# Sliding-window attention and dropless MoE on one core: another division of the queries, score groups issued in pairs, a third task list in three portions

## The chip, the cores and the metric

The kernel runs on one core of one Trainium2 chip. The metric is the device time of one execution in microseconds (us), taken as the median of several runs; before the change it was 678.85 us over five runs (677.37 to 681.30). A profile is one further execution, recorded by the hardware profiler. Engines are called by the profile's short names: PE is TensorE's matmul queue and PEld its weight loads, DVE is VectorE, ACT ScalarE, POOL GpSimd and SP SyncE. "L828" is line 828 of the kernel before.

## The reference

Attention with a window of 128 keys and a bias that falls with distance is followed by a mixture of eight experts, of which each token takes one. All data are float32: 8 batches, 8 heads, 576 positions, head size 64; 4608 tokens of width 512; experts with a hidden width of 1024.

```python
def _attn_ref(q, k, v):
    scores = scale * np.matmul(q, k.transpose(0, 1, 3, 2))
    bias = slopes[:, None, None] * (-np.abs(rel).astype(np.float32))[None, :, :]
    mask = (rel >= 0) & (rel < window)
    scores = np.where(mask, scores + bias[None], -1000000000.0)
    attn = np.exp(scores - np.max(scores, axis=-1, keepdims=True))
    attn = attn / (np.sum(attn, axis=-1, keepdims=True) + 1e-09)
    return np.matmul(attn, v)

def _moe_ref(x, w_gate, w1, w2):
    logits = x @ w_gate
    expert_idx = np.argmax(logits, axis=1)
    probs = softmax(logits)
    gate_w = probs[np.arange(N), expert_idx]
    for e in range(E):                       # rows sorted by expert
        h = np.maximum(x_sorted[lo:hi] @ w1[e], 0.0)
        y_sorted[lo:hi] = h @ w2[e]
    return gate_w[:, None] * y
```

## The kernel before

The work has two stages. In the first, attention runs over 16 *units*: a unit is one pair of heads of one pair of batches, and four units in a row (four pairs of heads) make up one pair of batches, called `bp` 0 to 3. Behind each pair of batches its tokens are routed: gate products, a choice of expert, and rows written to DRAM (`x_rows`) sorted later by a gather. In the second stage the experts' matmuls run, with a Strassen scheme. The order of the instructions on every engine is written out by hand: an engine works through its queue in the order in which the Python code issues, and waits where a semaphore isn't there yet.

A sequence of 576 positions has nine blocks of 64 keys, and a key block meets at most three query blocks (its own and the next two). For a unit the loop at L1389 takes four steps, `g` = 0 to 3; the step counter over all units is `i`. The pieces are:

- `scores(i)`: the score products of one step's key blocks (two blocks, or three at `g` = 3; L785, 16 or 24 passes of weight load and matmul), into one of two PSUM buffers `sp`; then ACT's exponentials (L794, L804) and DVE's product with the bias factors (L798), into one of six buffers `pe`. `scores_to(n)` issues groups up to number n, so scores run three (units 0 and 1) or four steps ahead of their use.
- `values(u, half, kbs)`: the products of probabilities and values (L828) for key blocks `kbs`, for one half of the queries. The halves are `QH`: query blocks 0 to 4 and 5 to 8. There is one PSUM buffer `at` for them, so a half's first product waits until the half before has been copied.
- `finish(u, half)`: ACT copies the half's context to `xT` (L845, L847); PE forms the row sums (L859) in a PSUM buffer `m`, and DVE adds them to `sumT` (L870), or ACT copies them there for the first pair of heads (L868). There are two `m` buffers, taken in turn by everything outside scores and values.
- `some()`: pops one portion of tasks. `behind(bp)` returns the list of portions for a finished pair of batches, and the loop appends it after the pair's last step. Its members: `gate` (L879, with DVE's sum L884 or L886), `turn` (a PE transpose L903 and ACT's copy L904), `scale_a` to `scale_c` and `count` (small DVE operations), `place` and `place2` (L990 to L1014), `ones_at` and `ones_at2` (one-hot tables on DVE, L1023, L1029, L1038), `enlist` (L1048). Rows of the later pairs are turned on PE (`row_turned`, L1067, with ACT's copy L1069 into one of four `xs` buffers) and written by POOL (`row_out`, L1076 and L1081). Rows of the first pair are transposed on DVE (`squares_turned`, L1118, into the same `xs` buffers) and written by POOL in four DMAs each (`squares_scaled` L1126, `squares_out` L1137), after `scales_squared` (L1096, L1104).
- For `bp` = 2 the last portion also gathers the first expert's rows (L1271), and the last unit's steps scale and turn them (`to_scale` L1283, `to_columns` L1296).

Loads of unit u + 2 are issued on SP, one in each step. Ahead of each stands a tiny DMA that reads `prob[i + 1]` (`no_earlier_than`, L638), so the load can't start before that score group has been made.

Of the kernel before, what the change touches and what calls it, by code (L numbers as in the profile page):

```python
# [458 lines left out]
def kernel(  # L459
# [22 lines left out]
    KB = P // 2  # L482
# [24 lines left out]
    with ExitStack() as fast:  # L507
# [67 lines left out]

        GC = 384
        LQ = 4 * P
        QH = [(0, 5 * KB), (5 * KB, 4 * KB)]

        ac = pool(att, "att_consts", 1)  # L580
        qk = pool(att, "qk", 3)
# [227 lines left out]
        def by_distance(x, kb, a, b):  # L809

            if kb == NK - 1:
                return x[:, 5 * KB :].rearrange("p (j x) -> p j x", j=1)
            return x.rearrange("p (j k x) -> p j k x", j=3, k=2)[:, a:b, kb % 2, :]

        def values(u, half, kbs):

            bp, hp = units[u]
            q0, qn = QH[half]
            if (u, half) not in at:
                at[u, half] = ps_a.tile([P, 2, 512], F32, name="at"), set()  # L820
            acc, begun = at[u, half]
            for kb in kbs:
                pe = prob[4 * u + min(kb // 2, 3)]
                lo, hi = max(q0, kb * KB), min(q0 + qn, (kb + 3) * KB)
                at_kb = (kb, lo // KB - kb, hi // KB - kb)
                for c in range(2):
                    for r in range(2):
                        nc.tensor.matmul(  # L828
                            acc[r * D : (r + 1) * D, c, lo - q0 : hi - q0].rearrange("p (j x) -> p j x", x=KB),
                            lhsT=v_sb[u][c * KB : (c + 1) * KB, kb, r * D : (r + 1) * D],  # L830
                            rhs=by_distance(pe[c * KB : (c + 1) * KB, r, :], *at_kb),
                            start=(c, r) not in begun, stop=True, skip_group_check=True,
                        )
                        begun.add((c, r))

        def finish(u, half):

            bp, hp = units[u]
            q0, qn = QH[half]
            if hp == 0 and half == 0:  # L840
                xT[bp] = xp.tile([P, HP, 2 * S], F32, name="xT")
                sumT[bp] = xp.tile([P, S], F32, name="sumT")
            acc = at.pop((u, half))[0]
            n = min(q0 + qn, LQ) - q0
            nc.scalar.copy(xT[bp][:, hp, : 2 * LQ].rearrange("p (b q) -> p b q", b=2)[:, :, q0 : q0 + n], acc[:, :, :n])  # L845
            if n < qn:
                nc.scalar.copy(xT[bp][:, hp, 2 * LQ :].rearrange("p (b q) -> p b q", b=2), acc[:, :, n:qn])  # L847
            sm = ps_m.tile([P, 512], F32, name="m")
            ops = []
            for kb in range(max(0, q0 // KB - 2), (q0 + qn) // KB):  # L850
                lo, hi = max(q0, kb * KB), min(q0 + qn, (kb + 3) * KB)
                ops.append((kb % 2, lo, hi, prob[4 * u + min(kb // 2, 3)], (kb, lo // KB - kb, hi // KB - kb)))
            if half == 0:
                ops.insert(0, (1, 0, KB, None, None))
            begun = set()
            for par, lo, hi, pe, at_kb in ops:
                for r in range(2):
                    j = 2 * r + par
                    nc.tensor.matmul(  # L859
                        sm[32 * j : 32 * j + 32, lo - q0 : hi - q0].rearrange("p (j x) -> p j x", x=KB),  # L860
                        lhsT=none[:] if pe is None else ind[:, hp, :],
                        rhs=fac[:, 0:1, :KB] if pe is None else by_distance(pe[:, r, :], *at_kb),
                        start=j not in begun, stop=True, skip_group_check=True,
                    )
                    begun.add(j)
            to = sumT[bp][:, q0 : q0 + qn]
            if hp == 0:
                nc.scalar.copy(to, sm[:, :qn])  # L868
            else:
                nc.vector.tensor_tensor(to, sm[:, :qn], to, op=ALU.add)  # L870
# [212 lines left out]
        def row(bp, t):  # L1083
            row_turned(bp, t)
            row_out(bp, t)
# [30 lines left out]
        def squares_turned(bp, t):  # L1116
            xs = squares(bp, t)
            nc.vector.transpose(  # L1118
                xs[:, :, :PD].rearrange("p k (h j) -> p k h j", h=HP),
                xT[bp][:, :, t * P : (t + 1) * P].rearrange("p h (k i) -> p k h i", k=NA),  # L1120
            )
# [218 lines left out]
        def behind(bp):  # L1340

            g3 = [lambda k=k: gate(bp, k) for k in range(3)]
            t3 = [lambda k=k: turn(bp, k) for k in range(3)]
            rs = [lambda t=t: row(bp, t) for t in range(TPB)]
            a, a2, b, b2, c, n, q, p, p2, o, o2, e = (
                [lambda f=f: f(bp)] for f in (
                    scale_a, scale_a2, scale_b, scale_b2, scale_c, count, scales_squared, place, place2, ones_at,
                    ones_at2, enlist,
                )
            )  # L1350
            if bp == 0:
                rt = [lambda t=t: squares_turned(bp, t) for t in range(TPB)]
                ro = [
                    lambda t=t: (squares_scaled(bp, t), squares_out(bp, t, nc.gpsimd)) for t in range(TPB)
                ]
                return [g3[0:1], g3[1:2], g3[2:] + t3[0:1], t3[1:], a, a2, b, b2, c + n, rt[0:1], q + p + rt[1:2],
                        p2 + rt[2:4] + ro[0:2], o + ro[2:4], o2, rt[4:6] + ro[4:5], e + rt[6:8] + ro[5:8]]
            rt, ro = ([lambda t=t, f=f: f(bp, t) for t in range(TPB)] for f in (row_turned, row_out))
            if bp == 1:
                last = [lambda: squares_turned(0, TPB - 1), lambda: squares_scaled(0, TPB - 1),  # L1360
                        lambda: squares_out(0, TPB - 1, nc.gpsimd)]
                return [g3[0:1], g3[1:2], g3[2:] + t3[0:1] + last, t3[1:], a + rt[0:1], a2 + rt[1:2], b + rt[2:3],
                        b2 + rt[3:4], c + n, [], p + ro[0:2], p2 + ro[2:4] + rs[4:5], o + rs[5:6], o2 + rs[6:7], rs[7:8],
                        e + rs[8:9]]
            return [g3, t3, a + a2, b + b2 + rt[0:1], c + n + rt[1:2], rt[2:4], p + p2 + ro[0:4], o + o2 + rs[4:6],
                    rs[6:9] + [early_holes], e + [early_table, lambda: gather(fixed[0], x_d[: 3 * 2 * S, :])]]

        tasks = []
# [1 line left out]
        def some():  # L1370
            if tasks:
                for f in tasks.pop(0):
                    f()
# [4 lines left out]
        def scores_to(n):  # L1378
            while scored[0] < min(n, NG):
                scores(scored[0])  # L1380
                scored[0] += 1
# [7 lines left out]
        for i in range(NG):  # L1389
            u, g = divmod(i, 4)  # L1390
            bp, hp = units[u]
            if u + 2 < len(units):
                no_earlier_than(prob[i + 1][0:1, 0, 0:1])
                load_part(u + 2, g)
            if u in (5, 6) and g % 2 == 1:
                d = 2 * (u - 5) + g // 2
                load_w1(fixed[0], w1_a, slice(d, d + 1))
            if i == 1:
                token_numbers()
                table_consts()  # L1400
            if i == 12:
                token_parts()

            ahead = i + (3 if u < 2 else 4)
            if g == 0:
                scores_to(ahead)
            if g == 0:
                values(u, 0, (0, 1))
                if u < HP - 1:
                    factors(u + 1)  # L1410
            elif g == 1:
                values(u, 0, (2, 3))
            elif g == 2:
                values(u, 0, (4,))
                finish(u, 0)
                some()
                scores_to(ahead)
                values(u, 1, (3, 4, 5))
            else:
                values(u, 1, (6, 7, 8))  # L1420
                finish(u, 1)
            if u in (10, 11):
                ws_tasks.pop(0)()
            if u == len(units) - 1 and g == 1:
                first = [t for _, t in prepare(fixed[0])]
                tasks.extend(first[:3])
            if g != 2:
                some()
            if g in (1, 3):
                scores_to(ahead)  # L1430
            if g == 3 and hp == HP - 1 and bp < BP - 1:
                tasks.extend(behind(bp))
# [250 lines left out]
        for i in range(len(groups)):  # L1683
            g = groups[i]
# [20 lines left out]
            ahead = []  # L1705
# [47 lines left out]
```

## Time and profile before

| | |
|---|---|
| median of five runs | 678.85 us (677.37 to 681.30) |
| the profiled execution | 678.02 us, span 676.3 us |
| granted TensorE clock | 0.999 |
| PE busy | 650.8 us, 96% |
| DVE, ACT, POOL busy | 362.0, 215.6, 238.9 us |
| DMA | 122.01 MB, 180 GB/s over the span |
| last score product starts, last value product of attention | about 163 and 169 us |

A row of the timeline gives the start, the duration, the engine, the line and operation, the tiles, how many instructions were merged, and in square brackets the idle time of the engine before it with what ended it ("issue" is none that the profile shows). A row of the stage windows gives the stretch, its length, then busy time and instruction count of PE, PEld, DVE, ACT and POOL, the granted clock, the DMA share and GB/s. Matmul durations include the pipeline's drain, so gaps on PE show more plainly in the weight loads' rows.

### The profile page before, as it was taken

What the parts mean: (1) busy time and instruction counts of PE and PEld (TensorE: products, weight loads), DVE (VectorE), ACT (ScalarE), POOL (GpSimd) and SP (SyncE); (2) the same over time, 40 slices, a digit from 0 to 9 for tenths busy, and PEclk for the clock granted to TensorE, in tenths of its full rate; (3) what the DMA queues carried; (4) which work ended last, traced back from release to release, by engine and by line L of the source; (5) the groups of instructions that cost most, each with busy time, mean ns of one, the idle gap of its engine ahead of it and who ended that gap; (6) DMA issues with size and microseconds to landing.
All of it is one profiled execution on the core that took longest, in us unless ns stands there. A gap on an engine that the chain in (4) does not pass through costs nothing.

```text
span 676.3 us, 14663 instructions
## 1 busy us (share of the span) xinstructions
PE 650.8 (96%) x6004; PEld 542.5 (80%) x6004; DVE 362.0 (54%) x727; ACT 215.6 (32%) x493; POOL 238.9 (35%) x372
## 2 busy tenths in 40 slices
PE   6899889999999999999999999999999999999995
PEld 5777768687788888978878887889788888878893
DVE  3345848776697768435633761484257436623510
ACT  5657557676331231023102311310231023113200
POOL 8000573215032571247026521732371266112020
PEclk9999999999999999999999999999999999999999
DMA  9876997965438944582386518444823664184010
GB/s 274 215 205 189 330 238 215 295 183 165 143 85 266 339 131 141 185 286 68 118 269 215 169 52 289 155 154 157 304 59 135 227 246 149 53 288 151 1 63 9
DMA packets 63167, 122.01 MB, mean 180 GB/s; under 512 B 5905, under 2 KB 29489, under 8 KB 63090
## 3 DMA queue, kind: packets, MB, share of 16 engines
q1 hardware_dynamic: 51138, 92.51, 43.0%
q0 software_dynamic: 10800, 27.58, 12.7%
q8 instruction: 49, 0.80, 0.5%
q10 hardware_dynamic: 1152, 0.88, 0.4%
q14 instruction: 28, 0.23, 0.1%
HBM read 101.79 MB, written 19.96 MB: 180 GB/s over the span
## 4 chain that ended last, share of the span: by engine, by line
PE 67%; issue 15%; POOL 6%; DVE 4%; DMA 2%; ACT 1%; SPq 0%; POOLq 0%; DVEq 0%; ACTq 0%
PE sp L785 4%; PE at L828 4%; PE pair1a L1558 4%; PE pair1b L1558 4%; PE pair0b L1501 4%; PE pair0a L1501 4%; PE pair0a L1558 4%; PE pair0b L1558 4%; PE pair2b L1501 4%; PE pair2a L1501 4%; POOL xg L1271 4%; PE pair1b L1501 3%; PE pair1a L1501 3%; PE pair2b L1558 3%; PE pair2a L1558 3%
## 5 line engine op out<-in xcount | busy, mean ns | idle before, releaser
L1271 POOL DMA_INDIRECT xg<-x_rows,p_idx x124 | 125.4, 1011 | 37.8 <-issue 37.2
L1581 POOL DMA_INDIRECT out_dram<-zo,s_idx x39 | 44.4, 1139 | 244.5 <-DVE zo L1572 142.8
L798 DVE TENSOR_TENSOR pe<-pe,fac 128x512 f32<-128x512 f32 x64 | 43.6, 687 | 45.6 <-ACT pe L794 45.6
L785 PE MATMUL sp<-q_sb,k_sb 64*64 64x192 f32 (+2 forms) x1152 | 55.9, 322 | 9.3 <-DMA q_sb<-in_qT_dram 5.0
L828 PE MATMUL at<-pe,v_sb 64*64 64x192 f32 (+2 forms) x1408 | 56.2, 287 | 2.9 <-issue 2.0
L828 PEld LDWEIGHTS at<-pe,v_sb 64*64 64x64 f32 x1408 | 47.0, 135 | 11.6 <-issue 4.6
L785 PEld LDWEIGHTS sp<-q_sb,k_sb 64*64 64x64 f32 x1152 | 40.6, 137 | 18.3 <-issue 7.6
L794 ACT ACTIVATE pe<-sp 128x512 f32<-128x512 f32 x64 | 38.5, 601 | 32.8 <-issue 18.5
L804 ACT ACTIVATE pe<-sp,mid 128x128 f32<-128x128 f32 x128 | 40.2, 374 | 0.0
L1512 ACT ACTIVATE h<-h 128x512 f32<-128x512 f32 x32 | 20.2, 630 | 38.6 <-DVE h L1511 38.6
L859 PE MATMUL m<-pe,ind 128*32 128x192 f32 (+2 forms) x704 | 29.7, 286 | 1.1 <-DVE sumT L870 0.9
L1137 POOL DMA_DIRECT2D x_rows<-xs x48 | 26.0, 549 | 9.7 <-POOL xs L1126 2.3
L1283 DVE TENSOR_TENSOR xn<-xg 128x512 f32<-128x512 f32 x39 | 26.2, 675 | 1.3 <-DMA xg<-x_rows,p_idx 0.7
L859 PEld LDWEIGHTS m<-pe,ind 128*32 128x32 f32 x704 | 23.1, 109 | 3.7 <-DVE sumT L870 1.0
L1299 DVE STREAM_TRANSPOSE xgT<-xn 128x512 f32<-128x512 f32 x31 | 22.0, 711 | 1.1
L845 ACT COPY xT<-at 128x640 f32<-128x640 f32 (+1 forms) x32 | 18.9, 591 | 9.4 <-PE at L828 6.6
L538 DVE TENSOR_TENSOR w2s<-w 128x512 f32<-128x512 f32 x16 | 11.0, 685 | 20.3 <-DMA w<-in_moe_w_dram 20.3
L1126 POOL COPY xs<-sq 128x16 f32<-128x16 f32 x10 | 2.6, 264 | 54.0 <-ACT sq L1104 54.0
L1613 PE MATMUL pair2a<-w,h 128*128 128x512 f32 x48 | 21.1, 592 | 0.0
L1501 PE MATMUL pair0a<-xgT,w 128*128 128x256 f32 x72 | 17.1, 380 | 0.0
L1501 PE MATMUL pair0b<-xgT,w 128*128 128x256 f32 x72 | 17.1, 380 | 0.0
L1558 PE MATMUL pair1a<-w,h 128*128 128x256 f32 x72 | 17.1, 380 | 0.0
(378 smaller groups left out, 1382.9 us busy)
## 6 DMA issues: line engine op xcount, KB each, us to landing
w<-in_moe_w_dram SPq DMA_DIRECT2D x29, 2048.0 KB, 7.8
k_sb<-in_kT_dram SPq DMA_DIRECT2D x15, 576.0 KB, 5.9
q_sb<-in_qT_dram SPq DMA_DIRECT2D x15, 576.0 KB, 5.4
v_sb<-in_v_dram SPq DMA_DIRECT2D x30, 288.0 KB, 5.9
x_rows<-xs POOLq DMA_DIRECT2D x16, 264.0 KB, 4.6
x_rows<-xs POOLq DMA_DIRECT2D x32, 66.0 KB, 5.6
x_rows<-xT SPq DMA_DIRECT2D x8, 264.0 KB, 5.9
w<-in_moe_w_dram SPq DMA_DIRECT2D x4, 512.0 KB, 9.6
```

The lines of the kernel that those rows point to most:

```text
L785: nc.tensor.matmul(by_distance(sp[c * KB : (c + 1) * KB, r, :GC], kb, 0, n), lhsT=k_sb[u][hs, c, kb * KB : (kb + 1) * KB], rhs=q_sb[u][hs, ...
L794: nc.scalar.activation(outer, sp[:, :, :GC].rearrange("p r (j x) -> p r j x", j=3)[:, :, 0:3:2, :], AF.Exp, scale=SCALE,)
L798: nc.vector.tensor_tensor(outer, outer, fac[:, h0 : h0 + 2, : 2 * w].rearrange("p r (j x) -> p r j x", j=2)[:, :, :, : 2 * KB], op=ALU.mult,)
L804: nc.scalar.activation(pe[:, r, inner], sp[:, r, inner], AF.Exp, bias=mid[:, h0 + r : h0 + r + 1], scale=SCALE,)
L828: nc.tensor.matmul(acc[r * D : (r + 1) * D, c, lo - q0 : hi - q0].rearrange("p (j x) -> p j x", x=KB), lhsT=v_sb[u][c * KB : (c + 1) * KB, ...
L859: nc.tensor.matmul(sm[32 * j : 32 * j + 32, lo - q0 : hi - q0].rearrange("p (j x) -> p j x", x=KB), lhsT=none[:] if pe is None else ind[:, ...
L1137: eng.dma_start(x_d[r0 : r0 + n * m, a * PW : (a + 1) * PW].rearrange("(k i) w -> i k w", i=TQ), xs[a * TQ : (a + 1) * TQ, p0 // TQ : p0 / ...
L1271: nc.gpsimd.indirect_dma_start(out=to, out_offset=None, in_=where, in_offset=bass.IndirectOffsetOnAxis(ap=idx, axis=0),)
L1283: nc.vector.tensor_tensor(xn[:], x, s.unsqueeze(3).to_broadcast([P, NA, HP, TQ]), op=ALU.mult)
L1501: nc.tensor.matmul(ps[:, f * 256 : (f + 1) * 256], lhsT=left[m][:, d, fb * P : (fb + 1) * P], rhs=right[m][:, d, :], start=(m in (1, 2, 5) ...
L1558: nc.tensor.matmul(ps[:, :256], lhsT=left[m][:, f, c * P : (c + 1) * P], rhs=right[m][:, f, :], start=(m in (1, 2, 5) and f == 0), stop=Tr ...
L1581: ins = nc.gpsimd.indirect_dma_start(out=out[:, :], out_offset=bass.IndirectOffsetOnAxis(ap=s_idx[:, g["c0"] + j : g["c0"] + j + 1], axis= ...
```

## The change

The queries are divided behind four blocks in place of five, so the first half needs key blocks 0 to 3 only and the second needs 2 to 8. `finish(u, 0)` moves from step 2 to step 1, ahead of that step's portion, and step 2's portion moves behind its scores and values. The score group of step 2 now directly follows that of step 1, as that of step 0 already followed that of step 3. In the list of the second pair (`bp` = 1) the last row of the first pair, left over in `last`, moves from the third portion to the first. The list of the third pair (`bp` = 2) gets three portions in place of two for the gate products and turns, so every later portion comes one step later.

```diff
-        QH = [(0, 5 * KB), (5 * KB, 4 * KB)]
+        QH = [(0, 4 * KB), (4 * KB, 5 * KB)]
...
-                return [g3[0:1], g3[1:2], g3[2:] + t3[0:1] + last, t3[1:], a + rt[0:1], a2 + rt[1:2], b + rt[2:3],
+                return [g3[0:1] + last, g3[1:2], g3[2:] + t3[0:1], t3[1:], a + rt[0:1], a2 + rt[1:2], b + rt[2:3],
                         b2 + rt[3:4], c + n, [], p + ro[0:2], p2 + ro[2:4] + rs[4:5], o + rs[5:6], o2 + rs[6:7], rs[7:8],
                         e + rs[8:9]]
-            return [g3, t3, a + a2, b + b2 + rt[0:1], c + n + rt[1:2], rt[2:4], p + p2 + ro[0:4], o + o2 + rs[4:6],
+            return [g3[0:2], g3[2:] + t3[0:1], t3[1:], a + a2, b + b2 + rt[0:1], c + n + rt[1:2], rt[2:4], p + p2 + ro[0:4], o + o2 + rs[4:6],
                     rs[6:9] + [early_holes], e + [early_table, lambda: gather(fixed[0], x_d[: 3 * 2 * S, :])]]
...
-            if g == 0:
+            if g % 2 == 0:
                 scores_to(ahead)
             if g == 0:
                 values(u, 0, (0, 1))
...
             elif g == 1:
                 values(u, 0, (2, 3))
+                finish(u, 0)
             elif g == 2:
-                values(u, 0, (4,))
-                finish(u, 0)
-                some()
-                scores_to(ahead)
-                values(u, 1, (3, 4, 5))
+                values(u, 1, (2, 3, 4, 5))
             else:
                 values(u, 1, (6, 7, 8))
                 finish(u, 1)
...
-            if g != 2:
-                some()
-            if g in (1, 3):
+            some()
+            if g % 2 == 1:
                 scores_to(ahead)
```

## The prediction

> **What bounds the kernel now.** I read the busy shares first, then the windows by stage, the waits of the weight loads, and the timeline of attention.
>
> ```profile
> PE 650.8 (96%) x6004; PEld 542.5 (80%) x6004; DVE 362.0 (54%) x727; ACT 215.6 (32%) x493; POOL 238.9 (35%) x372
> ...
> 70.00:85.00 15.00, 12.89 (x311) 10.79 (x310) 12.12 (x28) 8.71 (x24) 9.90 (x21) 1.00 1.05 325
> ...
> 175.00:190.00 15.00, 14.71 (x77) 12.79 (x76) 10.64 (x33) 6.08 (x12) 0.00 (x0) 1.00 0.24 91
> ...
> PEld sp L785 <- issue: 6.9, 14, 1.9
> PEld at L828 <- issue: 4.6, 9, 1.1
> PEld at L828 <- ACT xT L845: 2.5, 7, 0.4
> ```
>
> TensorE sets the end in every stage. After 173 us (experts) it has almost no gap, and the diff touches nothing there; what can change lies in attention, 4 to 173 us. A matmul's row includes its drain, so I read gaps from the weight loads. Between 30 and 175 us they wait 2.5 us for the context copies (L845), which is what the change is near. More, 11.5 us, is "issue": part is the 0.17 us between groups of another array shape, but seven of them stop in the middle of a group with no semaphore (ending at 22.84, 30.03, 35.45, 66.96, 73.46, 79.45, 84.64; 0.44 to 1.91 us, together 7.7). The instruction queue moves 49 packets, 0.80 MB, so 16 KB each, about 245 of the 12,008 PE instructions; from 66.96 to 73.46 lie 129 pairs of load and matmul. I read these as PE waiting for its next instruction packet behind data (DMA share 1.05 in that window).
>
> **1. The gap at the division, gain.** One unit without other tasks:
>
> ```profile
> 41.91 0.53 PEld L785 LDWEIGHTS sp<-q_sb,k_sb 64*64 64x64 f32 x16
> ...
> 42.08 0.70 ACT L845 COPY xT<-at 128x640 f32<-128x640 f32 x1
> ...
> 42.83 1.41 PEld L828 LDWEIGHTS at<-pe,v_sb 64*64 64x64 f32 x48 [0.39 <-ACT xT L845]
> ```
>
> The second half's values reuse the only context buffer, so they wait for the copy; row sums (0.9) and one score group (0.53) cover it and leave 0.39. After the change two score groups lie there: 0.53 more cover, and a copy of 512 instead of 640 elements (0.60 by the 128x512 copies of L904, against 0.70). ACT first has the exponentials of two groups to do, 1.0 us each by their spacing at 46.10 and 47.09, from 1.0 us after the pair of scores starts: copy done 3.8 us after it, values due at 1.31 + 1.14 + 0.75 + 1.06 = 4.3. The gap closes. (Units 1 and 2 have 0.86 us of factors on ACT ahead of the copy: 0.3 may stay.) SP issues the same DMAs in the same order, POOL too but for the gather of step 4. The same total of blocks is multiplied: per unit 88 value and 48 sum matmul passes before and after. The other copy grows from 0.48 to 0.60; sums and two scores (2.1) still hide it, and if not it costs 0.12 a unit.
>
> The gap stands in eight units (14.48, 34.36, 42.83, 62.06, 82.14, 95.80, 138.90, 160.97; 0.28 to 0.39, together 2.84). In units 0, 2, 5 and 7 a packet wait follows within some 5 us and takes the gain back: PE arrives 0.36 earlier at a packet that comes no earlier. Units 8, 12 and 14 are in the sums below. Left: unit 3, **-0.4**.
>
> *Rule against trace.* The Trainium skill, "Runtime: NRT & Kernel Launch", section "Instruction fetch mechanics", says that crossing a 16 KiB block is mostly hidden. Here 7.7 us were not. By the rule those four gaps are gained too, 1.4 us more; I follow the trace.
>
> **2. Unit 8, loss.** A portion at g = 2 stood after the fifth block and the first sums; now it stands after two scores and four blocks of values. Of the first pair the tenth portion there (scales squared, L1096) starts POOL's row writes: first copy at 71.74, then DMAs whose waits reach back eight DMAs. DVE's transposes of later rows wait for those landings, and PE for DVE:
>
> ```profile
> 87.63 0.71 DVE L1118 STREAM_TRANSPOSE xs<-xT 128x512 f32<-128x512 f32 x1 [1.90 <-DMA x_rows<-xs]
> ...
> 90.24 0.71 DVE L1118 STREAM_TRANSPOSE xs<-xT 128x512 f32<-128x512 f32 x1 [1.89 <-DMA x_rows<-xs]
> ...
> 91.58 0.34 PE L828 MATMUL at<-pe,v_sb 64*64 64x64 f32 x8 [0.52 <-DVE pe L798]
> ...
> 92.78 0.25 PE L859 MATMUL m<-fac,none 128*32 128x64 f32 x2 [0.86 <-DVE gs L884]
> ```
>
> The chain starts later by score 0.53 + values 1.14 + array change 0.17 = 1.85. Bounds: 0 (the chain takes it up elsewhere) and 3.5 (the packet wait that ended at 73.46 then falls ahead of L1096; by my count of pairs it falls just behind). I take 2.2. So the row 7 transpose moves from 90.24 to 92.4, and behind it on DVE two factor products and the first gate's sum; PE, now held by the second gate product, which needs the first one's PSUM buffer, goes on at 92.78 + 2.2. From there before needed 6.11 to the next pair of scores (98.89). After: second gate 1.06, two scores 1.23, values 1.14, third gate 0.47, turn 0.45, values 1.02, sums 0.92, two turns 0.75 = 7.04, since fewer pieces were done ahead of the wait: +0.93. The last row's transpose, two portions earlier, waits on DVE for row 4's landing with the second gate's sum behind it; the unit's context copy waits for that transpose before (95.06) and after. It ends before PE's values ask. Its 8 DMAs stay last on POOL. **+3.1**.
>
> *Rule against trace.* "DMA: Bandwidth & Descriptors", section "Anatomy of one DMA — SWDGE (gpsimd) path", fits 2.0 us plus bytes over 436 GB/s: 2.15 us for the 66 KB of a piece. The row of these DMAs says 5.6. By the rule no transpose would wait and this loss would be nothing; I follow the row.
>
> **3. Units 10 and 11.** Placing (L990) waits 0.82 for DVE in unit 10; two pieces later it finds its input ready. But in unit 11 the sums now stand between rows 5 and 6, so row 6 needs row 5's copy, which ACT delays (it stood 2.03 us for a row buffer at 119.35). Between -0.8 and +0.2: **-0.3**.
>
> **4. Third pair.** Three portions shift all later ones by one slot. Unit 12: the 0.39 gap and 0.24 of the turns' wait go; two more array changes (0.35) and 0.2 for the first turn, which needs ACT's copy of the sums, come. Slot 8 (unit 14, g = 0) gets the one-hot tables:
>
> ```profile
> 151.97 0.60 DVE L1023 TENSOR_TENSOR at_col<-cols_b,rc 128x432 bf16<-128x432 bf16 x1
> ...
> 152.60 1.13 DVE L1029 TENSOR_TENSOR oc<-at_col,tok 128x432 bf16<-128x432 bf16 x2
> ...
> 153.64 1.35 DVE L1038 TENSOR_TENSOR gsr<-cols_b,rc 128x1152 bf16<-128x1152 bf16 x1
> ...
> 166.91 0.69 DVE L1283 TENSOR_TENSOR xn<-xg 128x512 f32<-128x512 f32 x1 [0.40 <-DMA xg<-x_rows,g_idx]
> ```
>
> These 3.0 us now precede the first sums' add on DVE. Counted from the pair of scores: factor products end at 3.35, tables 6.4, add 6.85. PE has finished row 6 at 5.0; row 7 needs the sums' buffer (two `m` buffers alternate) and waits 1.85. Behind it: row 8, the hole product (0.35 for row 7's copy), both scores, all values. In unit 15 no scores are left to cover the division: 0.5. F0 waits 0.1, array changes 0.15. The gather goes out about 1.7 us later, but the product that uses it moves behind four blocks of values: the wait of 0.76 goes, with 0.38 (row 8) and 0.34 (unit 14's gap). +3.5 - 2.1 = **+1.4**; with the tables done earlier -0.4, with ACT later +2.5.
>
> **Sum:** -0.4 + 3.1 - 0.3 + 1.4 = +3.8. The profiled execution took 678.02 (span 676.3 and 1.7 around it), 0.8 under the median; 681.8 there, **682.7** as a median.
>
> **Rivals.** *A, as summed*, 0.55; own range 680.4 to 685, more above than below since the 3.5 of step 2 lies upward. *B, the row chain takes up its delay*, 0.17: POOL stood 2.30 us at 79.70, which the trace puts down to DVE's at_col; if that, not the landing, held it, 2.2 goes: 680.5. Against it: that DMA's wait names the first row's landing as well, and 7.2 us is the longest landing in the view. *C, faster*, 0.15: in unit 8 DVE never waits for a landing. The price of that place is then its old waits, 0.86 + 0.99 gained; with eight gaps 2.8, L990 0.8, minus 1.4 for the third pair: 673.8 to 675. It decides once landings stay under about 3.5 us (2.9 is the shortest seen); against it stands a median of 5.5 from 60 to 100 us. *D, packets later still*, 0.13: the loads are paced by probabilities, which now come in twos, so two loads start together; if each of the seven packet waits grows by 0.8, +5.6: 688.
>
> **Chances.** A measurement here can tell some 0.5% (3.4 us). A lies beyond in 0.41 and within in 0.14; B is within; C faster; D slower. Faster 0.15, same 0.31, slower 0.54. Leaving out most of C and part of D gives 677 to 687.5.
>
> **What would show it.** No wait on L845 ahead of values in units 3 and 5; L1126's first copy about 2 us later against L828 of unit 6, and the second gate product of unit 8 waiting 3 us or more on L884; a row turn (L1067) of unit 14 waiting near 1.9 us on sumT L870. Wrong if DVE's transposes stop waiting for landings, or if packet waits shrink or move. After 175 us nothing should differ.

## The result, and the profile after

The changed kernel took 682.7 us, the median of 30 runs (678.3 to 688.26), beside 679.07 us for the kernel before (56 runs): a ratio of 1.0055, 95% interval 1.0041 to 1.0069. So it is slower by half a per cent, and the prediction's 682.7 us is what came. The sum behind it is another matter: two of its terms were wrong, and one cause was not in it at all. (Here and below, a ratio leaves out runs of over 1.5% above the fastest of their kernel: four of twelve in one kernel, named there, and none elsewhere.) The profiled execution took 682.47 us (span 680.7; 678.02 and 676.3 before).

The busy shares of the kernel after, from the page:

```profile
PE 653.3 (96%) x6004; PEld 544.7 (80%) x6004; DVE 363.4 (53%) x727; ACT 216.5 (32%) x493; POOL 238.9 (35%) x372
```

The same two stretches as before, in the windows view (stretch, length, busy time and instructions of PE, PEld, DVE, ACT, POOL, granted clock, DMA share, GB/s):

```profile
70.00:85.00 15.00, 12.35 (x287) 10.25 (x290) 12.34 (x28) 6.78 (x19) 9.95 (x21) 0.92 1.05 314
175.00:190.00 15.00, 14.70 (x91) 11.21 (x90) 9.97 (x23) 5.84 (x11) 0.00 (x0) 1.00 0.42 141
```

The number to see is 0.92. Before, the clock column of this stretch read 1.00. And the waits of the weight loads between 30 and 180 us (wait, sum, times, longest):

```profile
PEld at L828 <- issue: 5.0, 15, 0.8
PEld m L859 <- issue: 4.0, 3, 2.4
PEld m L879 <- DVE gs L884: 3.6, 2, 2.7
PEld m L1067 <- DVE sumT L870: 2.3, 2, 1.7
...
PEld at L828 <- ACT xT L845: 0.6, 1, 0.6
```

The wait for the context copies (L845) went from 2.5 us in seven places to 0.6 in one, the last unit. In its place stand two long ones: 2.7 us at a gate product and 1.7 us at a row turn.

Where the time went is read from the start of the scores that open each unit:

| start of | before | after | difference |
|---|---|---|---|
| unit 4 | 45.10 | 45.14 | +0.04 |
| unit 8 | 85.36 | 84.21 | -1.15 |
| unit 9 | 98.89 | 100.69 | +1.80 |
| unit 12 | 129.51 | 131.28 | +1.77 |
| unit 14 | 152.69 | 152.84 | +0.15 |
| unit 15 | 163.24 | 167.65 | +4.41 |
| experts (first pair0a) | 173.45 | 177.72 | +4.27 |
| end of span | 676.3 | 680.7 | +4.4 |

Units 8 (16.48 us in place of 13.53) and 14 (14.81 in place of 10.55) lose most. Unit 3 loses 2.0 us to packet waits, stops in the middle of a group that no semaphore explains (shown below); the others together gain. Unit 8 in the timeline after, DVE and the weight loads:

```profile
86.86 0.71 DVE L1118 STREAM_TRANSPOSE xs<-xT 128x512 f32<-128x512 f32 x1 [2.28 <-DMA x_rows<-xs]
...
89.48 0.71 DVE L1118 STREAM_TRANSPOSE xs<-xT 128x512 f32<-128x512 f32 x1 [1.92 <-DMA x_rows<-xs]
91.29 0.69 DVE L884 TENSOR_TENSOR gs<-m,sumT 128x512 f32<-128x512 f32 x1
...
92.03 0.16 PEld L879 LDWEIGHTS m<-xT,wgd 128*32 128x32 f32 x8 [2.71 <-DVE gs L884]
...
93.04 2.23 PEld L785 LDWEIGHTS sp<-q_sb,k_sb 64*64 64x64 f32 x32 [0.86 <-issue]
...
95.34 1.46 PEld L828 LDWEIGHTS at<-pe,v_sb 64*64 64x64 f32 x32
```

The chain is the one foretold: landing, transpose, the first gate's sum, then the second gate product. But look at the two rows behind the wait. 32 passes of scores take 2.23 us; elsewhere in the same trace the same 32 take 1.18. The 32 of values take 1.46; elsewhere 0.97. Unit 14 shows the same, DVE first, then the weight loads:

```profile
156.09 0.60 DVE L1023 TENSOR_TENSOR at_col<-cols_b,rc 128x432 bf16<-128x432 bf16 x1
...
157.78 1.35 DVE L1038 TENSOR_TENSOR gsr<-cols_b,rc 128x1152 bf16<-128x1152 bf16 x1
159.04 0.41 DVE L870 TENSOR_TENSOR sumT<-m,sumT 128x256 f32<-128x256 f32 x1
```

```profile
159.51 0.86 PEld L1067 LDWEIGHTS m<-ident,xT 128*128 128x128 f32 x8 [1.72 <-DVE sumT L870]
160.97 0.32 PEld L1184 LDWEIGHTS m<-acc,ones_sq 128*128 128x128 f32 x2 [0.61 <-ACT xs L1069]
161.31 2.22 PEld L785 LDWEIGHTS sp<-q_sb,k_sb 64*64 64x64 f32 x32
163.61 1.46 PEld L828 LDWEIGHTS at<-pe,v_sb 64*64 64x64 f32 x32
```

Unit 3, shown before for its gap of 0.39 us, has none ahead of its values now, and a packet wait of 1.39 us ahead of the last sums:

```profile
39.94 0.97 PEld L785 LDWEIGHTS sp<-q_sb,k_sb 64*64 64x64 f32 x24
40.91 1.84 PEld L828 LDWEIGHTS at<-pe,v_sb 64*64 64x64 f32 x56
...
44.47 0.48 PEld L859 LDWEIGHTS m<-pe,ind 128*32 128x32 f32 x15 [1.39 <-issue]
```

The granted clock in windows says why units 8 and 14 run slowly behind their waits. The trace records the clock's changes. Three stretches of 3.41 us run at half speed, beginning at 82.70, 92.94 and 161.21 us, all on one grid of 3.413 us (3 and 20 steps apart). Here is each with the stretch ahead of it:

```profile
79.29:82.70 3.41, 1.48 (x46) 1.13 (x39) 2.69 (x4) 1.29 (x5) 2.70 (x7) 1.00 1.04 354
82.70:86.11 3.41, 3.25 (x39) 2.42 (x42) 1.41 (x3) 0.23 (x1) 1.95 (x5) 0.50 1.11 278
89.53:92.94 3.41, 0.91 (x8) 0.16 (x8) 3.06 (x5) 0.26 (x1) 3.12 (x7) 1.00 0.63 120
92.94:96.35 3.41, 3.41 (x56) 2.73 (x56) 1.39 (x2) 2.07 (x6) 3.12 (x7) 0.50 0.95 288
157.79:161.21 3.42, 1.56 (x13) 1.09 (x10) 1.67 (x3) 1.48 (x4) 1.84 (x5) 1.00 0.60 233
161.21:164.62 3.41, 3.41 (x54) 2.77 (x57) 1.16 (x4) 1.72 (x5) 1.83 (x4) 0.50 0.49 144
```

Ahead of each, PE was busy for 43%, 27% and 46% of a step. The kernel before has no such stretch in its profile until PE's work ends. Hence two theories for the experiments. **W**, as predicted: the loss is the waits themselves. **C**: a wait long enough to leave PE under about half busy in one step of the grid (a guess from the three steps above) also halves the clock of the next step, and that is a large part of the loss.

### The profile page after: what moved, and what is told of

Same layout as the page of the kernel before. It is cut to its first block, busy times and chain, and to the rows that moved or that the text cites. A ratio compares the mean times of both kernels' runs of the same rounds, so it can differ in the third digit from the quotient of the medians.

```text
span 680.7 us, 14667 instructions
## 1 busy us (share of the span) xinstructions
PE 653.3 (96%) x6004; PEld 544.7 (80%) x6004; DVE 363.4 (53%) x727; ACT 216.5 (32%) x493; POOL 238.9 (35%) x372
## 4 chain that ended last, share of the span: by engine, by line
PE 58%; issue 25%; POOL 9%; DMA 4%; DVE 3%; ACT 1%; POOLq 0%; DVEq 0%; ACTq 0%
PE pair1a L1554 4%; PE pair1b L1554 4%; PE pair0b L1497 4%; PE pair0a L1497 4%; PE pair0a L1554 4%; PE pair0b L1554 4%; PE pair2b L1497 4%; PE pair2a L1497 4%; DMA x_rows<-xs 4%; POOL xg L1271 3%; PE pair1b L1497 3%; PE pair1a L1497 3%; PE pair2b L1554 3%; PE pair2a L1554 3%; PE pair0a L1609 2%
## 5 line engine op out<-in xcount | busy, mean ns | idle before, releaser
L798 DVE TENSOR_TENSOR pe<-pe,fac 128x512 f32<-128x512 f32 x64 | 43.3, 688 | 43.8 <-ACT pe L794 43.7
L785 PEld LDWEIGHTS sp<-q_sb,k_sb 64*64 64x64 f32 x1152 | 42.5, 143 | 17.5 <-issue 5.0
L845 ACT COPY xT<-at 128x512 f32<-128x512 f32 x32 | 19.2, 600 | 14.0 <-PE at L828 8.8
```

What stands on the lines that cost most here:

```text
L785: nc.tensor.matmul(by_distance(sp[c * KB : (c + 1) * KB, r, :GC], kb, 0, n), lhsT=k_sb[u][hs, c, kb * KB : (kb + 1) * KB], rhs=q_sb[u][hs, ...
L798: nc.vector.tensor_tensor(outer, outer, fac[:, h0 : h0 + 2, : 2 * w].rearrange("p r (j x) -> p r j x", j=2)[:, :, :, : 2 * KB], op=ALU.mult,)
```

## The experiments

Three chips served the runs below; each ratio is against the kernel before on the same chip. On one of them (the stops, and the two kernels with the sums moved) the kernel before takes 679.96 us, close to the first result's 679.07. On the other two it takes 730.59 and 729.41. There PE has long waits in the experts' stage (one of 11.1 us for DVE in the kernel before itself, where its first profile has none of over 1 us), and short stops near 165 us (five of 0.5 to 1.2 us from 163.7 to 167.3 in the same trace). The changed kernel itself ran for the first result only. Where a ratio from another chip is set against its 1.0055, the same ratio is assumed for it there.

### The price of a stop: the same stops, empty and filled

Where PE is otherwise full, in the experts' stage, 28 stops were put into the kernel before. PE makes one product, ACT copies it seven times, and PE waits for the last copy. `w` and `w2` are weights already in use; the empty kernel has 0 where the filled one has 8:

```diff
+        hold = wk_pool.tile([P, 256], mybir.dt.bfloat16, name="hold")
+        def stall(still):
+            a = ps_m.tile([P, 512], F32, name="m")
+            b = ps_m.tile([P, 512], F32, name="m")
+            nc.tensor.matmul(a[:, :256], lhsT=ident[:], rhs=still, start=True, stop=True)
+            for _ in range(7):
+                nc.scalar.copy(hold[:], a[:, :256])
+            for _ in range(8):
+                nc.tensor.matmul(b[:, :256], lhsT=ident[:], rhs=still, start=True, stop=True)
+            nc.tensor.matmul(b[:, :256], lhsT=hold[:, :P], rhs=hold[:], start=True, stop=True)
...
             for m, k in ORDER:
+                if m in (6, 3) and g is not fixed[0]:
+                    stall(w[:, 0, :256])
```

Empty:

> The kernel before, with 28 stops put into the experts' stage (four for each of the seven further experts), where PE otherwise has next to no gaps: PE makes one product, ACT copies it seven times (some 2.1 to 2.6 us by 0.37 us for a 128x256 copy and the two hand-overs), and PE waits for the last copy. Theory W: each costs its own length, 28 x (2.4 + 0.3) = some 70 us, the clock stays near 1. Theory C (under half busy in one 3.41 us stretch, the next at half clock, up to 1.7 us each): some 15 to 22 of the 28 are followed by a half-clock stretch, so 25 to 37 us more than its companion in which PE has work during the stop.

Filled:

> The same 28 stops, but PE gets eight products that nothing needs (1.7 us of PE) in each, while ACT makes its copies. W: the stop ends when ACT is done, so the time is that of the companion without the products, or more if the products outlast the copies. C: no half-clock stretch, 25 to 37 us less than the companion.

Measured: 835.51 us empty (1.2281, 1.223 to 1.2331) and 801.57 us filled (1.1802, 1.1753 to 1.185). One empty stop in the weight loads' timeline:

```profile
276.64 0.41 PEld L1449 LDWEIGHTS m<-w,ident 128*128 128x128 f32 x2
280.39 0.10 PEld L1454 LDWEIGHTS <-hold 128*128 128x128 bf16 x1 [3.35 <-ACT hold L1451]
280.39 1.94 PEld L1574 LDWEIGHTS pair0a<-w2s,hs 128*128 128x128 f32 x8
282.42 3.00 PEld L1574 LDWEIGHTS pair0b<-w2s,hs 128*128 128x128 f32 x8
285.44 1.70 PEld L1574 LDWEIGHTS pair2a<-w2s,hs 128*128 128x128 f32 x8
```

and the same stop, filled:

```profile
272.01 0.41 PEld L1449 LDWEIGHTS m<-w,ident 128*128 128x128 f32 x2
272.44 3.43 PEld L1453 LDWEIGHTS m<-w,ident 128*128 128x128 f32 x16
275.90 0.10 PEld L1454 LDWEIGHTS <-hold 128*128 128x128 bf16 x1
276.11 1.60 PEld L1574 LDWEIGHTS pair0a<-w2s,hs 128*128 128x128 f32 x8
```

The stops are nearly equally long, 3.75 us from the first row to the one on `hold` empty and 3.89 filled; over all 28 the means are 4.34 and 4.41 (longer than I had estimated). Behind the empty one a group of eight takes 3.00 us in place of 1.70. The clock record of the empty kernel has 26 half-speed steps behind 22 of the 28 stops, that of the filled kernel none in the stops' stage. The filled kernel does 224 products more and is 33.9 us faster: 33.9 / 26 = **1.3 us for a half-speed step**, where PE is the bound. W expected no gain from filling and is refuted as the whole story for such stops.

### The two waits of the changed kernel, filled

```diff
+        def filler(n):
+            if not held:
+                held.append(ps_s.tile([P, 2, 512], F32, name="sp"))
+            for _ in range(n):
+                products(scored[0], held[0])
...
-                    rs[6:9] + [early_holes], ...
+                    rs[6:7] + [lambda: filler(3)] + rs[7:9] + [early_holes], ...
...
+            if u == 8 and g == 1:
+                filler(3)
             some()
```

> The changed kernel, plus PE work that nothing needs: three repeats of the next score group's products (48 passes, some 1.6 us) into its PSUM buffer, which the real products overwrite, ahead of the second gate product of unit 8 and between rows 6 and 7 of unit 14. They lie inside the two waits of 2.7 us (L879 on gs) and 1.7 us (L1067 on sumT). Theory W (the loss is the waits themselves, as the prediction summed it): the waits end when they ended, so 682.7 us, no change against the changed kernel, and a granted clock like its own (0.9915 as a mean of its runs). Theory C (a stretch in which PE is under half busy halves the clock of the next 3.41 us, at about 1.5 us each): the half-speed stretches behind these two places go, clock about 0.995, the scores behind the gate take 1.2 us again in place of 2.2, and the time falls by 2 to 3 us, to about 680.

Measured: 1.005 of before (1.002 to 1.0081) on a chip of the second kind. By the time alone, W's forecast of no change stands, and C's 1.0015 lies just outside the interval. The profile shows what the filling did in its two places. In the weight loads' timeline of units 8 and 14 the gate is L895, scores L798, values L844, row turns L1083:

```profile
94.84 0.16 PEld L895 LDWEIGHTS m<-xT,wgd 128*32 128x32 f32 x8 [1.39 <-DVE gs L900]
95.83 1.18 PEld L798 LDWEIGHTS sp<-q_sb,k_sb 64*64 64x64 f32 x32 [0.84 <-issue]
97.03 0.97 PEld L844 LDWEIGHTS at<-pe,v_sb 64*64 64x64 f32 x32
...
160.59 0.86 PEld L1083 LDWEIGHTS m<-ident,xT 128*128 128x128 f32 x8 [0.28 <-issue]
162.06 0.30 PEld L1200 LDWEIGHTS m<-acc,ones_sq 128*128 128x128 f32 x2 [0.61 <-ACT xs L1085]
162.38 1.18 PEld L798 LDWEIGHTS sp<-q_sb,k_sb 64*64 64x64 f32 x32
163.57 0.98 PEld L844 LDWEIGHTS at<-pe,v_sb 64*64 64x64 f32 x32
```

Scores are back at 1.18, values at 0.97. From the second gate product to unit 9 the filled kernel takes 7.05 us (94.84 to 101.89), the changed one 8.66 (92.03 to 100.69); from row 7 to unit 15 6.53 (160.59 to 167.12) against 8.14. Both differ by 1.61: the half-speed steps, in the very places. The trace also has what sets against this gain: a packet wait ahead of unit 4 is 2.76 us long (1.39 in the changed kernel's trace), and unit 8 still opens with a half-speed step, at 85.55 us behind a packet wait of 2.36. Whether the 96 added pairs of load and matmul, themselves most of an instruction packet, bring such waits in most runs isn't shown.

### The third pair: two portions again, or the tables one step later

```diff
-            return [g3[0:2], g3[2:] + t3[0:1], t3[1:], a + a2, ...
+            return [g3, t3, a + a2, ...
```

> The changed kernel with the third pair's gate products and turns in two portions again, so every later portion one step earlier. Step 4 of the prediction with W: 1.4 us of the loss goes, 681.3. With C: the wait of 1.7 us on sumT in unit 14 goes and with it a half-speed stretch in most runs: 680 to 680.5. Rival, the third pair costs nothing: 682.7.

Measured: 1.0066 (1.0033 to 1.0099), no gain. The wait and the half-speed step (at 151.59 us) are still there, one unit earlier:

```profile
148.45 0.42 PEld L1067 LDWEIGHTS m<-ident,xT 128*128 128x128 f32 x4
151.08 0.42 PEld L1067 LDWEIGHTS m<-ident,xT 128*128 128x128 f32 x4 [2.21 <-DVE sumT L870]
151.69 2.23 PEld L785 LDWEIGHTS sp<-q_sb,k_sb 64*64 64x64 f32 x32 [0.19 <-issue]
```

So the third portion isn't what costs. The cost comes from the sums that now stand between the portions of steps 0 and 1: they hold one of two `m` buffers until DVE, which has the earlier portion's work first, adds them. In both orders the portion at step 0 is one with much DVE work, and step 1's second `m` user waits. So the next run moves the tables, and leaves the sums where they are:

```diff
-  ..., o + o2 + rs[4:6],
-                    rs[6:9] + [early_holes], ...
+  ..., rs[4:6],
+                    rs[6:8] + o + o2 + rs[8:9] + [early_holes], ...
```

> The changed kernel with the third pair's one-hot tables (3.0 us of DVE) moved from the portion of unit 14's step 0 to that of step 1, behind rows 6 and 7, so the first sums' add no longer stands behind them. W: the wait of 1.72 us of row 7 goes and nothing else: about 681.0. C: the same, and the half-speed stretch that follows it in most runs goes too: about 680, with the scores at unit 14's end back at 1.2 us from 2.2. Rival: the tables now delay the hole's sum or the enlisting (L1048) by as much: 682.7.

Measured: 0.9997 (0.9969 to 1.0025), so 0.6% under the changed kernel's ratio, some 4 us, with an interval of about 2 either way. Row 7 waits 0.21 us on `sumT` where it waited 1.72, and the scores behind it take 1.18 us:

```profile
157.90 0.42 PEld L1067 LDWEIGHTS m<-ident,xT 128*128 128x128 f32 x4 [0.21 <-DVE sumT L870]
...
159.69 1.18 PEld L785 LDWEIGHTS sp<-q_sb,k_sb 64*64 64x64 f32 x32
```

Unit 14 takes 11.49 us (14.81). W's 1.7 us lies just outside that interval, C's 2.7 inside. The gain of unit 14 is 3.3 us, about the wait and the half-speed step together.

### Unit 8: row buffers of their own

Rows 4 to 8 of the first pair go to the tile of the weight sums, unused until unit 10:

```diff
+                if bp == 0 and t > 3:
+                    if "ws" not in fixed[0]:
+                        fixed[0]["ws"] = ws_pool.tile([P, 3, DB // 2, F // 2], F32, name="ws")
+                    flat = fixed[0]["ws"].rearrange("p a b c -> p (a b c)")
+                    w = NA * PW
+                    xs_of[bp, t] = flat[:, (t - 4) * w : (t - 3) * w].rearrange("p (k w) -> p k w", k=NA)
```

> The changed kernel with rows 4 to 8 of the first pair in a tile of their own (the weight sums' tile, free until unit 10) in place of the four row buffers, so that no transpose of them on DVE waits for a landing. Step 2 of the prediction (landing, then DVE, then the first gate's sum, then PE) with W: the second gate product of unit 8 waits under 1 us in place of 2.7, time about 680. With C: also no half-speed stretch in unit 8: about 678.5 to 679. Rival, the wait isn't the landings': still over 2 us at L879, about 682.7.

Measured: 1.001 (0.9984 to 1.0035), 0.45% under the changed kernel's ratio. The gate product waits for nothing but the usual pauses, and DVE (the transpose is L1125 here) has rows 6 and 7 done without a landing:

```profile
85.67 1.29 DVE L1125 STREAM_TRANSPOSE ws<-xT 128x512 f32<-128x512 f32 x2
```

Unit 8 takes 12.20 us, though, as in the changed kernel, a packet wait ahead of it (2.36 us) has put its first 2 us at half speed. The landings were the cause of unit 8's wait, then. The 4.3 us won in the unit are W's 2.7 and the half-speed step's 1.6; the time, 3 us less by the ratios with about 2 either way, is too uncertain to tell the two theories apart.

### The sums behind the scores, alone and with the row buffers

`finish` is cut into its copy and its sums:

```diff
             elif g == 1:
                 values(u, 0, (2, 3))
-                finish(u, 0)
+                copied(u, 0)
...
             some()
             if g % 2 == 1:
                 scores_to(ahead)
+            if g == 1:
+                summed(u, 0)
```

> The changed kernel with step 1's pieces in another order: values, context copy, portion, scores, and only then the row sums of the first half (they stood ahead of the portion). The sums then no longer take one of the two m buffers between two portions. W: the waits of 1.72 and 0.61 us in unit 14 go, the gate's 2.71 us in unit 8 shrinks by the 1.2 us of the scores that come ahead: about 679.2 on the chip of the first result, 0.9 to 1.0 times before. C: the half-speed stretch of unit 14 goes as well, that of unit 8 in some runs: about 677.5, 0.998 of before. Rival, the sums' wait moves with them behind the scores: 682.7, 1.0055 of before.

> That order, and rows 4 to 8 of the first pair in the weight sums' tile. W: the rest of unit 8's wait goes too, about 677.7 or 0.998 of before. C: no half-speed stretch but behind a packet wait: about 676, 0.9955 of before. Rival, unit 8's wait is not the landings': as the kernel with the new order alone.

Measured: 1.0012 (0.9984 to 1.004), mean clock 0.9939, for the order alone; 0.9985 (0.9955 to 1.0016), mean clock 0.9955, with the row buffers. Unit 14 takes 11.5 us in both, unit 8 13.18 and 11.50. The long waits of both places went, in the first kernel that of unit 8 as well. The order alone lies 0.4% under the changed kernel's ratio, with the row buffers it is 0.7%, each with about 0.3 either way: with both waits gone the whole loss is gone. Between W and C the times don't decide. W's 1.0002 and 0.998 lie inside the intervals, C's 0.998 just outside the first and 0.9955 at the edge of the second; the plain medians, 681.84 and 677.99 us, lie above both theories' figures (679.2 and 677.5, then 677.7 and 676). In the first kernel packet waits of 1.65, 3.12 and 3.17 us (ending 64.42, 78.04, 85.84), in the second of 2.48 twice and 1.96 (13.99, 45.21, 74.47) took back part of what was won.

### Packet waits: the weights' loads later

The kernel before, with its loads of the first weights in units 9 and 10 (their sums in 11 and 12):

```diff
-            if u in (5, 6) and g % 2 == 1:
-                d = 2 * (u - 5) + g // 2
+            if u in (9, 10) and g % 2 == 1:
+                d = 2 * (u - 9) + g // 2
...
-            if u in (10, 11):
+            if u in (11, 12):
                 ws_tasks.pop(0)()
```

> The kernel before with the loads of the first expert's first weights (four of 0.5 MB) issued in units 9 and 10 in place of 5 and 6, and their sums on DVE in units 11 and 12 in place of 10 and 11. If PE's mid-group waits are instruction packets held up behind data: those between 60 and 86 us (1.13, 1.03, 1.59 and 0.44 before) shrink to under 1.5 us together, and the time falls by 2 to 4 us, 0.994 to 0.997. If they come with the instructions whatever the data do: as before, 1.000.

Measured: 1.0014 (0.9987 to 1.0042), no gain. The mid-group waits from 57 to 84 us did go: 3.8 us in the kernel before, 4.8 in the kernel before on this chip, none of over 0.3 us here, at a DMA share of 0.84 from 60 to 85 us in place of 1.02. Units 5 to 7 took 25.4 us in place of 28.5 and 29.8. Unit 8 gave it back: it began at 83.57 and ended at 98.97 (85.36 and 98.89 in the first profile, 85.07 and 96.95 in the kernel before on this chip), with waits for the gate sums as before and a half-speed step in it. Units 11 and 14, too, were some 2 us longer; unit 11 now has weight sums on DVE that stood in unit 10.

The same loads moved in the kernel with both changes above, to units 9 and 10 and to units 12 and 13:

> The changed kernel with the sums behind the scores, rows 4 to 8 of the first pair in a tile of their own, and the loads of units 5 and 6 in units 9 and 10. Both causes at once (packet waits of 60 to 86 us gone, no stops of over 1.7 us in units 8 and 14): 0.993 to 0.995 of before. If packets are late whatever the data do: as without the later loads, 0.9985.

> The same with those loads in units 12 and 13, where the DMA engines have most room, and the sums of weights on DVE in units 14 and 15. If data hold up packets: 0.992 to 0.995, unless DVE's eight sums (0.68 us each) hold up the one-hot tables and the gathered rows' scaling at the end of attention, by up to 2 us: then 0.996 to 0.998.

Measured: 0.9971 (0.9941 to 1.0001) and 0.9933 (0.9894 to 0.9972). The second figure rests on the eight lowest of twelve runs. Over all twelve the medians, 726.51 and 729.41, say 0.4%, and with runs from 718.56 to 736.0 beside 723.37 to 733.01 it isn't shown that it is faster than the kernel before. Packet waits are still in its trace, 3.00 us ending at 40.36 and 2.35 at 85.08, the latter at a DMA share of 0.77. So the later loads don't remove them reliably.

### The kernel before against itself

> The kernel before itself, unchanged, for the granted clock of each of its runs. C: its mean clock lies 0.003 or more above the 0.9915 that the changed kernel had as a mean over 32 runs (0.0025 for each half-clock stretch of 3.41 us in 680), which at some 1.3 us a stretch is most of the 3.75 us between the two. W: the two clocks agree within 0.001, and the time is made of waits alone.

Measured: 0.9989 (0.9962 to 1.0017), a mean clock of 0.9704. It ran on a chip of the other kind, so its clock can't be set against the changed kernel's. The number that can came with the stops: 23 runs of the kernel before, on the chip like the first, had a mean clock of 0.9952. The changed kernel's 0.9915 (32 runs) is 0.0037 less. A half-speed step takes 0.0025 off the mean of 680 us, so that is 1.5 steps a run. At 1.3 to 1.6 us each I estimate some 1.9 to 2.4 us of the 3.7 between the two kernels; it is an upper estimate, since a step whose delay a following wait takes up costs nothing. The profiled run with three steps had more than the mean, that of before with none less.

## Why the prediction came out right, and where its steps failed

| step | predicted | profile | of that, half speed |
|---|---|---|---|
| 1 and 2, to the start of unit 9 | +2.7 | +1.80 | 1.6 |
| 3, units 9 to 11 | -0.3 | -0.03 | 0 |
| 4, unit 12 to the experts | +1.4 | +2.50 | 1.6 |
| sum | +3.8 | +4.27 | 3.2 |

The total came right by luck. Without the half-speed steps the profiled differences come to +1.1, under a third of the sum; the clock, at which the prediction didn't look, made up the rest. Over the mean of the runs its share is smaller, at most the 1.9 to 2.4 us above.

**The gap at the division** closed: no wait on L845 in units 3 and 5, one of 0.56 us in unit 15, where 0.5 was expected. What became of it was misjudged. Unit 3's gain went into packet waits (0.81 and 1.39 us in that unit); units 4 to 7 ended 1.15 us early, and unit 8 took all of it, since its pace is set by the rows' landings.

**Unit 8** was right in its chain and wrong in its cause. "The chain starts later by 1.85" failed: the first copy ran at 71.09, 0.65 earlier than before, since PE had come to unit 6 early (63.58, 64.33 before) and met no packet wait on its way to L1096, where there had been one of 1.13 us. Row 7's transpose stood at 89.48, not 92.4; chain length is the same, 18.4 us from first copy to this transpose (18.5 before). Counted from the start of unit 6 and without that packet wait, L1096's products did come later, but by 1.2 us (5.74 for 4.51) and not 1.85. The wait was 2.71 us because PE came early to a chain that the landings pace. "7.04 from there to the next pair" is 7.05 in the kernel with that wait filled: the 0.93 for less work done ahead is confirmed. In the changed kernel it was 8.66, and the 1.61 between them is the clock, which the sum didn't have. So -0.75 for the wait's end (92.03 for 92.78), +0.94, +1.61: +1.80. The first half-speed step, at 82.70, made the unit's opening scores take 2.31 us in place of 1.40, but the wait behind them took that up. Of the foretold +3.1, +0.9 came as reasoned, the later start not at all.

**Units 10 and 11**: the place wait fell from 0.82 to 0.28, and row 6 waited 1.36 us on row 5's copy; inside the bounds, at no net.

**The third pair**: row 7 waited 1.72 us (1.85), the hole 0.61 (0.35), the first turn 0.56 (0.2), unit 15's values 0.56 (0.5). Without the half-speed step the part comes to +0.9, near the +1.4. But it was put down to the third portion, and with two portions it stays: the mechanism (tables ahead of the sums' add, two buffers) held, its owner is the moved `finish`.

**What was missing**: the clock. The trace of before couldn't show the drop: PE was busy for 57% or more in each step of its grid from 9 us to the end of attention (59% from 25.82 to 29.23 us), with the clock at 1.00. But a forecast of waits of 2 and 3 us was reason to ask for it. The Trainium skill, "TensorE: Matmul & The Clock Gate", Part 1, describes this gate: a free-running window of 3413 ns, half rate after an idle one. The grid and the half rate agree with the trace. The condition is weaker here: the steps ahead of the slow ones were 27 to 46% busy, and a wait of 2.36 us was enough. By the Trainium skill's sentence in the same page's section on oscillation, which sets the bar at PE-idle gaps of over about 3.4 us, no stretch of the changed kernel's attention would have slowed: its longest gap is 2.71 us.

**The rivals**: B held that POOL's stop of 2.30 us was DVE's doing; after, the same stop (1.84 us at 78.77) is put down to the landing, and there was no delay for the chain to take up. D was right that the packet waits would move (after, they end at 13.31, 23.31, 38.77, 44.47, 71.38 and 82.86), wrong that they would grow: 7.7 us, as before. That a crossing is mostly hidden, as the Trainium skill has it ("Runtime: NRT & Kernel Launch", "Instruction fetch mechanics"), doesn't fit the trace after either. Instruction packets land at 65.50, 72.06 and 77.87 us before and at 70.14 and 81.34 after. Waits put down to packets end 1.2 to 1.6 us behind each of these landings, at 66.96, 73.46, 79.45, 71.38 and 82.86. What delays a packet is open: less data removed the waits of one stretch in one kernel and not in another.

## What to carry to other kernels

Before a change that makes a wait of PE longer, lay the wait against the step of the clock. A half-speed step followed 15 of the 23 waits of over 2 us that the fourteen traces have between 10 and 165 us, and 22 of the 28 empty stops, which are 3.75 to 5.3 us long. It cost 1.3 to 1.6 us where PE was the bound behind it. Products that nobody needs, put into the wait, saved that in the stops; in attention they cleared both places, and no time was won. A gain ahead of a place that is paced by something else (here row landings, an absolute time) is only a longer wait there; cost moves against that place, not against the work before it. And where two buffers are taken in turn by all users, a user moved between two portions makes the next ones wait for the first portion's work on DVE.

## What the runs showed that had not been expected

The clock's rule can be put in numbers, from all fourteen traces: whole steps of the grid that ran at full speed and began later than 9 us into the span. Of 71 with PE busy for under 0.40 of the time, 71 were followed by a step at half speed; from 0.40 to 0.55, 23 of 50; above, 4 of 2659, all four at 163 to 173 us on the slower chips. PE's busy share is modelled, so the edge may be sharper than this. Ahead of 9 us the clock's record has no half-speed step, though 32 passes of scores take 2.26 us there (at 6.51 in the trace after), as in the slow steps. The grid lies differently in each trace, so the same wait is dear in one run and cheap in the next (row 7's wait of 1.92 us in the kernel with the row buffers was followed by none). In the changed kernel's 32 runs, from 678.3 to 688.26 us, time and mean clock go against each other with a correlation of only -0.44, so the clock is one source of that spread among others. And chips differ: the same kernel takes 680 us on one and 728 to 731 on two others, nearly all of it in the experts' stage (502.9 us from its start to the end of the span before, 544.7 there).
